# Band attention and a GELU layer on one core: seven-product second layer for two more chunks, f16 scores for three units, 64-row products that subtract the maxima

## The chip, the cores and the metric

The kernel runs on one core of one Trainium2 chip. The metric is the device time of one execution in microseconds (us). A profile gives the span from the first to the last instruction.

## The reference

Attention over 4 batches, 8 heads, 768 positions and 64 dimensions, in which a query sees the keys within 15 positions of its own and one summary key for each block of 32 (the block's maximum, with the mean of the block's values). The output is fed to a two-layer network.

```python
k_sum = k.reshape(B, H, nb, block, D).max(axis=3)
v_sum = v.reshape(B, H, nb, block, D).mean(axis=3)
scores_all = np.concatenate([scores_l_m, scores_s], axis=-1)
scores_all = scores_all - np.max(scores_all, axis=-1, keepdims=True)
a = np.exp(scores_all)
a = a / (np.sum(a, axis=-1, keepdims=True) + 1e-09)
x = np.ascontiguousarray(attn_out.transpose(0, 2, 1, 3)).reshape(B * S, H * D)
h = x @ w_in                                   # 3072 x 512 by 512 x 2048
g = 0.5 * h * (1.0 + erf(h * inv_sqrt2))
return (g @ w_out).astype(np.float32)          # 3072 x 2048 by 2048 x 512
```

## The kernel before

The 3072 tokens are 12 chunks of 256. A chunk's attention is done in two units (24 in all) of 4 heads by 256 queries. An operand that must be exact to more than f16 is split into a high and a low f16 part, and a product is then three f16 products (high by high, high by low, low by high). ScalarE makes the high parts (`*_hi`), VectorE the low parts (`*_lo`), as a subtraction.

Attention of unit u: `scores` (or `f_scores`, with f32 operands; units 0 to 5) multiplies keys and queries, `evac` or `add_mask` brings the scores to SBUF, `maximum` finds the maximum over the 128 partitions on GpSimd, and the maximum is subtracted. That is `shift` (L789) on VectorE, or, for units 0 to 3, `m_shift` (L733) on TensorE: products that add minus the maximum to the scores still lying in PSUM. `exponent` or `m_exponent`, `sums` (denominators), `values`, and the `norm_*` steps follow, and `x_hi`, `x_lo` split the result, the input of the network. For `scores` the keys are split by `s_k_hi` and `k_lo` (L723), the queries by `s_q_hi` and `q_lo` (L728), and the block maxima by `prep_k_end` (L523) and `k_sums`; for `f_scores` ScalarE copies the keys into one f32 tile (`k_pack`).

First layer: chunks 0 to 3 with `phase1` (L908; 24 products of 256 columns a step), and chunks 4 to 11 in pairs (batch "b" = 2 to 5 is chunks 2b and 2b+1) by `sp` (L962), Strassen's seven products instead of eight. Second layer: `phase2` (L1023; 12 products of 512 columns for a quarter of the 2048 rows and 128 tokens). For b = 5 alone (chunks 10 and 11) the second layer is done in seven products too: `so` (L1169), whose left operands are sums of the GELU outputs (`h_sum`, `h_hi`, `h_lo`) and whose right operands are sums of parts of `w_out` (`t_sum`, `t_hi`, `t_lo`).

The weights arrive as raw 64-bit numbers. VectorE turns each of 8 pieces of `w_in` and 8 of `w_out` into f32 in three steps (`wi_bits`, `wo_bits`: L386, L391, L395), and then makes the low part: `wi_lo` (L424), `wo_lo` (L484). `phase1` of column block i needs `wi_lo i`; `phase2` of quarter q needs `wo_lo 2q` and `wo_lo 2q+1`, and the chunk's `g_lo`.

The order of the work on every engine and of the DMAs (all on SP's queue) is a list written out in the source, `ORDER`; each name is a method and its arguments, and each engine executes its own instructions in that order. Steps `fill` are products of ones whose result nobody reads: 14 of three products each, and 16 more products at the start. Tiles of a tag rotate through a number of buffers that the pool hands out in turn.

Of the kernel before, what the change touches and what calls it, by code (L numbers as in the profile page):

```python
# [82 lines left out]
0, wi_bits 2 0, evac 2, load_ind, wi_bits 2 1, fetch_vt 0, sum_vt 0, norm_cross 0, norm_rec 0, maximum 2, fetch_vt 1,
norm_spread 0, m_shift 1, m_exponent 1, fetch_vt 2, load_v 0, sum_vt 1, sum_vt 2, wi_bits 2 2, wi_hi 2, wi_lo 4,
k_pack 3, m_shift 2, fill 12, fetch_w_in 3 3, wi_lo 5, wi_lo 2, wi_bits 3 0, load_v 1, mean_vt, wi_bits 3 1, f_sums 1,
s_load_vs 0, f_values 0, norm_mult 0, m_exponent 2, f_mask 3, load_q 3, f_scores 3, s_load_vs 1, norm_take 1, wi_bits
3 2, x_hi 0, x_lo 0, norm_cross 1, norm_rec 1, f_values 1, fill 13, evac 3, f_sums 2, norm_spread 1, norm_mult 1,
norm_take 2, fetch_w_in 1 1, wi_hi 3, x_hi 1, x_lo 1, fetch_w_out 1 5, norm_cross 2, wi_bits 1 0, norm_rec 2, phase1 0
4, wo_bits 1 0, wi_bits 1 1, load_q 6, maximum 3, m_shift 3, s_q_hi 6, wo_bits 1 1, wi_bits 1 2, phase1 0 2, fetch_k 2
1, prep_k 2 1, load_v 2, m_exponent 3, load_vs 2, wi_hi 1, fetch_w_in 7 3, norm_spread 2, q_lo 6, phase1 0 5, f_values  # L90
2, load_v 3, gelu 0 5, g_hi 0 5, wi_lo 1, load_vs 3, fetch_k 1 3, f_mask 4, wo_bits 1 2, gelu 0 2, load_k 4, g_hi 0 2,
norm_mult 2, k_pack 4, f_sums 3, gelu 0 4, norm_take 3, load_q 4, norm_cross 3, prep_k 1 3, wi_bits 7 0, phase1 0 1,
f_values 3, wi_lo 3, wi_bits 7 1, load_v 4, wo_hi 1, fetch_k 1 2, f_scores 4, x_hi 2, fetch_k 1 1, evac 4, norm_rec 3,
norm_spread 3, g_hi 0 4, prep_k 1 2, gelu 0 1, phase1 0 0, x_lo 2, norm_mult 3, x_hi 3, fetch_w_in 6 2, prep_k 1 1,
f_mask 5, load_vs 4, x_lo 3, g_lo 0 4, g_lo 0 5, fetch_w_out 0 4, fetch_w_out 3 5, wi_bits 6 0, phase1 0 3, maximum 4,
shift 4, wo_lo 1, load_k 5, wi_bits 6 1, g_hi 0 1, g_lo 0 1, gelu 0 0, g_hi 0 0, g_lo 0 0, phase1 1 4, fetch_v 1 2,
load_q 5, gelu 0 3, fetch_k 1 0, phase1 1 5, exponent 4, g_hi 0 3, wi_bits 7 2, f_values 4, gelu 1 5, wo_bits 0 0,
wi_bits 6 2, f_sums 4, g_hi 1 5, g_lo 1 5, wi_hi 7, k_pack 5, wo_bits 0 1, norm_take 4, wi_lo 7, phase1 1 1, load_v 5,
gelu 1 1, g_hi 1 1, g_lo 1 1, wi_hi 6, phase1 1 0, wi_lo 6, prep_v 1 2, load_vs 5, gelu 1 4, f_scores 5, phase1 1 7,
norm_cross 4, gelu 1 0, g_hi 1 0, evac 5, g_hi 1 4, g_lo 0 3, load_k 6, s_k_hi 6, norm_rec 4, wo_bits 0 2, maximum 5,  # L100
norm_spread 4, prep_k 1 0, g_lo 1 0, load_v 6, wo_bits 3 0, fetch_w_out 2 4, phase1 1 6, wo_hi 0, wo_bits 3 1, phase1
1 3, gelu 1 7, phase1 0 7, wo_lo 0, phase2 0 0, shift 5, gelu 1 3, g_hi 1 3, wo_bits 3 2, fetch_w_out 5 5, g_lo 1 3,
norm_mult 4, wo_bits 2 0, exponent 5, f_sums 5, prep_k_end 1 0, f_values 5, gelu 1 6, wo_bits 2 1, load_q 7, norm_take
5, wo_bits 2 2, k_lo 6, g_hi 1 7, g_lo 1 7, wo_hi 3, k_sums 1 0, wo_bits 5 0, wo_lo 3, phase1 0 6, g_lo 0 2, gelu 0 6,
g_hi 0 6, wo_bits 5 1, wo_hi 2, wo_lo 2, fetch_w_out 4 4, f_mask 6, wo_bits 4 0, wo_bits 4 1, norm_cross 5, norm_rec
5, phase1 1 2, gelu 0 7, wo_bits 4 2, wo_hi 4, wo_bits 5 2, wo_hi 5, prep_k_end 1 1, wo_lo 4, wo_lo 5, g_lo 1 4,
scores 6, fetch_v 1 0, phase2 0 1, phase2 0 3, norm_spread 5, load_k 7, s_k_hi 7, phase2 0 2, fetch_v 1 1, phase2 0 5,
g_hi 0 7, fetch_w_out 6 4, x_hi 4, fetch_w_out 7 5, x_lo 4, norm_mult 5, s_q_hi 7, prep_v 1 1, evac 6, maximum 6,
phase2 0 4, load_mask, x_hi 5, x_lo 5, load_v 7, f_mask 7, q_lo 7, gelu 1 2, k_sums 1 1, shift 6, exponent 6, phase1 2
3, g_lo 0 6, wo_bits 6 0, phase1 2 1, load_q 9, k_lo 7, gelu 2 3, wo_bits 7 0, wo_bits 6 1, scores 7, g_hi 1 2, g_lo 1  # L110
2, wo_bits 6 2, wo_bits 7 1, gelu 2 1, s_q_hi 9, wo_hi 6, g_lo 0 7, wo_lo 6, phase1 2 0, load_k 9, wo_bits 7 2, q_lo
9, phase1 2 4, s_k_hi 9, k_lo 9, fetch_v 1 3, gelu 2 0, g_hi 2 0, s_p_hi 6, wo_hi 7, wo_lo 7, phase1 2 6, load_q 11,
load_k 8, phase2 0 6, fetch_k 2 2, prep_v 1 0, g_hi 1 6, g_lo 2 0, s_q_hi 11, prep_v 1 3, q_lo 11, p_lo 6, phase2 0 7,
store 0 0, phase2 1 0, fetch_v 2 1, load_vs 6, load_q 8, evac 7, maximum 7, load_vs 7, s_k_hi 8, gelu 2 6, put 0 0,
g_lo 1 6, prep_v 2 1, sums 6, k_lo 8, fetch_k 2 0, gelu 2 4, g_hi 2 4, v_hi 6, scores 9, norm_take 6, phase2 1 2,
phase2 1 4, prep_k 2 2, shift 7, v_hi 7, v_lo 6, values 6, store 0 1, fetch_k 2 3, g_lo 2 4, g_hi 2 1, prep_k 2 0,
phase1 2 5, s_q_hi 8, q_lo 8, add_mask 9, v_lo 7, scores 8, exponent 7, s_p_hi 7, norm_cross 6, phase2 1 6, p_lo 7,
load_v 8, prep_k 2 3, put 0 1, g_hi 2 6, load_k 11, s_k_hi 11, add_mask 8, load_vs 8, v_hi 8, k_lo 11, norm_rec 6,
norm_spread 6, sums 7, norm_mult 6, x_hi 6, norm_take 7, v_lo 8, phase1 2 2, maximum 9, shift 9, load_q 10, maximum 8,
shift 8, store 1 0, prep_k_end 2 1, values 7, norm_cross 7, norm_rec 7, scores 11, exponent 8, x_lo 6, exponent 9,  # L120
s_q_hi 10, phase2 1 1, load_v 9, norm_spread 7, load_vs 9, gelu 2 5, load_k 10, load_v 11, phase2 1 3, g_lo 2 1,
add_mask 11, load_vs 11, norm_mult 7, g_hi 2 5, g_lo 2 6, s_p_hi 8, p_lo 8, g_hi 2 3, g_lo 2 3, x_hi 7, phase1 2 7,
s_k_hi 10, phase2 1 5, x_lo 7, v_hi 9, maximum 11, phase1 3 0, v_lo 9, gelu 2 7, wt_add 1 0, wt_add 1 1, wt_add 1 2,
wt_hi 1, k_lo 10, sums 8, shift 11, values 8, s_p_hi 9, q_lo 10, norm_take 8, norm_cross 8, load_v 10, gelu 3 0, g_hi
3 0, wt_lo 1, fetch_k 3 1, load_q 12, load_vs 10, norm_rec 8, phase1 3 4, phase2 1 7, wt_add 5 0, p_lo 9, phase1 3 1,
norm_spread 8, norm_mult 8, put 1 0, g_lo 3 0, gelu 2 2, exponent 11, scores 10, wt_add 5 1, fetch_k 3 2, g_hi 2 2,
g_lo 2 2, prep_k 3 1, x_hi 8, store 1 1, wt_add 5 2, g_hi 2 7, g_lo 2 7, gelu 3 4, prep_k 3 2, values 9, wt_hi 5, sums
# [1216 lines left out]
```

## Time and profile before

| | |
|---|---|
| time, median of 3 runs | 576.7 us (575.52 to 577.2) |
| profiled execution, span | 574.3 us; its time is not recorded apart from its span |
| TensorE (PE) busy | 569.0 us, 99% of the span, 5826 products |
| VectorE (DVE) busy | 458.4 us, 80% |
| ScalarE (ACT) busy | 379.8 us, 66% |
| GpSimd (POOL) busy | 88.7 us, 15% |
| granted TensorE clock | 0.999 in the mean |

A product's listed duration is longer than the distance to the next one's start, as products are pipelined: busy times of single products must not be added, the distances of their starts may be. For VectorE the same holds to a smaller degree. The chain of waits is followed back from the last instruction, and names at every moment the work on which the end hung.

### The profile page before, as it was taken

The numbers are of one execution on the slowest core, as the hardware profiler recorded it, in microseconds if no ns is written. First come the engines' busy times: TensorE is split into PE (matmuls) and PEld (weight loads), VectorE is DVE, ScalarE is ACT, GpSimd is POOL, SyncE is SP. The second block draws the span as 40 slices with busy tenths as digits, with TensorE's granted clock in tenths as the row PEclk, the third lists the DMA queues.
The fourth block names the chain that finished last, engine by engine and source line by source line (L and its number), as shares of the span: only waits on it lengthen the run. The fifth ranks groups of instructions, "written<-read, shape, count | busy, mean of one in ns | idle before, by whom it ended". The sixth has DMA issues, their size and how long they took to land.

```text
span 574.3 us, 13533 instructions
## 1 busy us (share of the span) xinstructions
PE 569.0 (99%) x5826; PEld 389.8 (68%) x5826; DVE 458.4 (80%) x617; ACT 379.8 (66%) x642; POOL 88.7 (15%) x42
## 2 busy tenths in 40 slices
PE   9999999999999999999999999999999999999997
PEld 4457887485677565777755676665667756667886
DVE  4899999998999798988888677687556675678863
ACT  3486777666679667877987778774677843456431
POOL 2432340202422020203122220130400000000000
PEclk9999999999999999999999999999999999999999
DMA  8967955736433422342332231132020000000002
GB/s 322 395 238 250 342 175 196 274 116 198 159 115 99 141 79 71 115 121 76 103 93 66 72 105 56 60 98 78 23 63 1 21 19 18 1 20 1 2 1 91
DMA packets 28652, 64.27 MB, mean 112 GB/s; under 512 B 2736, under 2 KB 7600, under 8 KB 28592
## 3 DMA queue, kind: packets, MB, share of 16 engines
q1 hardware_dynamic: 28592, 63.41, 33.5%
q8 instruction: 45, 0.74, 0.5%
q14 instruction: 15, 0.12, 0.1%
HBM read 55.34 MB, written 6.29 MB: 107 GB/s over the span
## 4 chain that ended last, share of the span: by engine, by line
PE 95%; DVE 4%; issue 1%; ACT 0%; POOL 0%; DVEq 0%; ACTq 0%; POOLq 0%
PE psy L986 15%; PE pso L1034 12%; PE pso L1035 12%; PE pso L1036 12%; PE psz L986 7%; PE psh L915 4%; PE psh L917 4%; PE psh L916 4%; PE psx L986 4%; PE pso_y L1199 4%; PE psv L838 3%; PE pss L756 3%; PE pss_x L1199 2%; PE pso_fill L337 2%; PE pss L688 1%; PE pso_fill_s L337 1%
## 5 line engine op out<-in xcount | busy, mean ns | idle before, releaser
L785 POOL PARTITION_ALL_REDUCE m<-s x23 | 77.4, 3370 | 303.5 <-DVE s L776 80.9
L1034 PE MATMUL pso<-w_out_h,gg 128*128 128x512 f16 x320 | 121.5, 380 | 0.0
L1035 PE MATMUL pso<-w_out_l,gg 128*128 128x512 f16 x320 | 121.3, 379 | 0.0
L1036 PE MATMUL pso<-w_out_h,gg 128*128 128x512 f16 x320 | 121.3, 379 | 0.0
L986 PEld LDWEIGHTS <-wt 128*128 128x128 f16 x768 | 74.4, 98 | 13.6 <-issue 1.1
L916 PE MATMUL psh<-xos,ww 128*128 128x256 f16 x256 | 69.8, 273 | 0.6 <-DVE xos L895 0.6
L915 PE MATMUL psh<-xos,ww 128*128 128x256 f16 x256 | 69.9, 273 | 0.0
L917 PE MATMUL psh<-xos,ww 128*128 128x256 f16 x256 | 69.8, 273 | 0.0
L986 PE MATMUL psy<-xos,wt 128*128 128x256 f16 x576 | 69.3, 273 | 0.0
L986 PEld LDWEIGHTS <-ww 128*128 128x128 f16 x576 | 55.4, 98 | 11.7 <-issue 0.4
L1036 PEld LDWEIGHTS <-gg 128*128 128x128 f16 x320 | 31.3, 98 | 37.8
L1034 PEld LDWEIGHTS <-gg 128*128 128x128 f16 x320 | 31.3, 98 | 33.2 <-issue 0.8
L1035 PEld LDWEIGHTS <-gg 128*128 128x128 f16 x320 | 31.3, 98 | 31.5
L1018 DVE SCALAR_TENSOR_TENSOR gg<-g,gg 128x512 f16<-128x512 f32 x48 | 34.7, 731 | 11.5 <-ACT gg L1014 11.4
L997 ACT ACTIVATE ww<-psy 128x512 f32<-128x512 f32 x48 | 28.1, 587 | 23.7 <-PE psy L986 23.4
L1041 ACT ACTIVATE ot<-pso 128x512 f32<-128x512 f32 x20 | 11.8, 592 | 29.3 <-PE pso L1036 29.3
L1014 ACT ACTIVATE gg<-g 128x512 f16<-128x512 f32 x48 | 29.4, 625 | 2.7 <-PE pso L1035 2.0
L1004 DVE TENSOR_TENSOR g<-psz,ww 128x512 f32<-128x512 f32 x24 | 16.4, 682 | 18.5 <-PE psz L986 15.8
L1011 ACT ACTIVATE g<-g 128x512 f32<-128x512 f32 x36 | 22.3, 623 | 10.8 <-DVE g L1004 10.7
L915 PEld LDWEIGHTS <-ww 128*128 128x128 f16 x256 | 25.0, 98 | 6.3 <-issue 2.2
L917 PEld LDWEIGHTS <-ww 128*128 128x128 f16 x256 | 25.0, 98 | 3.7 <-issue 0.7
L916 PEld LDWEIGHTS <-ww 128*128 128x128 f16 x256 | 25.0, 98 | 3.4
(152 smaller groups left out, 1189.5 us busy)
## 6 DMA issues: line engine op xcount, KB each, us to landing
v<-in_vw_dram SPq DMA_DIRECT2D x24, 512.0 KB
k<-in_kd_dram SPq DMA_DIRECT2D x20, 320.0 KB
...
```

Source lines behind the costliest of these rows:

```text
L785: nc.gpsimd.partition_all_reduce(out_ap=self.m32, in_ap=self.s32, channels=P, reduce_op=bass_isa.ReduceOp.max)
L915: nc.tensor.matmul(ph[:, e, :], wh, xh, start=(k == 0), stop=False)
L916: nc.tensor.matmul(ph[:, e, :], wh, xl, start=False, stop=False)
L917: nc.tensor.matmul(ph[:, e, :], wl, xh, start=False, stop=(k == NCC - 1))
L986: nc.tensor.matmul(ps[:, e, :], ws, xx, start=(first and e == 0 and k == 0 and m == 0), stop=(k == 1 and m == 2), skip_group_check=True,)
L997: nc.scalar.activation(snaps[b, q, n], split8(acc[b, q, "y"]), AF.Copy)
L1014: nc.scalar.activation(g_part(o // 2, q, 0, slice(o % 2, 4, 2)), g32t[b, q, o], AF.Copy, scale=SC_G)
L1018: nc.vector.scalar_tensor_tensor(out=g_part(o // 2, q, 1, fs), in0=g32t.pop((b, q, o)), scalar=SC_G, in1=g_part(o // 2, q, 0, fs), op0=ALU ...
L1034: nc.tensor.matmul(p, gh, w_out_h[:, f, :], start=(f == 0), stop=False)
L1035: nc.tensor.matmul(p, gh, w_out_l[:, f, :], start=False, stop=False)
L1036: nc.tensor.matmul(p, gl, w_out_h[:, f, :], start=False, stop=(f == NFC - 1))
L1199: nc.tensor.matmul(ps[:, j, :], g, ww_, start=(first and e == 0 and k == 0), stop=(e == 1 and k == 2), skip_group_check=True,)
```

## The change

The second layer of chunks 8 and 9 (b = 4) is done by `so` as well, so `L2` is now a pair, and the methods take b as an argument. For b = 4 the sums of the GELU outputs lie in free rooms (`s_room`), the row halves of its "y" result in two PSUM tiles, and the sum of `w_out` number 1 is written in place over the part of `w_out` that `so` does not read. Units 3 to 5 use `scores` with f16 parts; units 3 to 5 then use `shift` (before, 4 and 5 did), and `m_shift` stays for units 0 to 2, with 64 rows of minus 1/64 instead of one row of minus 1. Tiles of ten tags take the buffer that a list (`SLOTS`) names. `ORDER` is written anew, with 11 fills instead of 14.

```diff
-L2 = 5
+L2 = (4, 5)
...
+class Slots:
...
+        if bufs > 1 and tag in SLOTS:
+            left = self.left.setdefault(tag, iter(SLOTS[tag].replace("\n", "")))
+            return self.pool.tile(shape, dtype, tag=f"{tag}_{next(left)}", bufs=1, name=name)
...
-            nc.gpsimd.memset(neg_1, -1.0)
+            nc.gpsimd.memset(neg_1, -1.0 / D)
...
-                row, sl = slice(e * D, e * D + 1), slice(e * QCOLS, (e + 1) * QCOLS)
+                rows, sl = slice(e * D, (e + 1) * D), slice(e * QCOLS, (e + 1) * QCOLS)
                 nc.tensor.matmul(
-                    self.halves[e], neg_1[row].broadcast_to([1, P]), self.m32[row, sl],
+                    self.halves[e], neg_1[rows].broadcast_to([D, P]), self.m32[rows, sl],
...
-    def a_part(q, m, z):
+    def s_room(q, m):
...
+    def a_part(b, q, m, z):
...
+        if b == L2[0]:
+            room, i = s_room(q, m), z * 2 * CH
...
     def t_room(q, n, z):
+        if n == 1:
+            return b_part(q, 0, 1, z)
...
-    def so(n, q, j):
+    def so(b, n, q, j):
...
+        key = (b, y, j) if y == "y" else (b, y)
...
+                acc[key] = ps_d.tile([P, CH], F32, tag="psd", name=f"psd_y_{b}") if j else (
+                    ps_o.tile([P, DM], F32, tag="pso", name=f"pso_y_{b}")[:, :CH])
```

Counted over the whole lists, these steps change in number: `phase2` 80 to 64, `so` 56 to 112, `h_hi` and `h_lo` 28 to 56 each, `h_sum` 16 to 32, `sg_hi` and `sg_lo` 48 to 32 each, `o_sum` 4 to 8, `scores` 18 to 21, `f_scores` 6 to 3, `k_lo` and `q_lo` 18 to 21 each, `prep_k_end` 6 to 8, `shift` 20 to 21, `m_shift` 4 to 3, `k_pack` 6 to 3, `fill` 14 to 11. `sp`, `phase1`, `t_sum`, `t_hi`, `t_lo`, `maximum`, `wi_*`, `wo_*` keep theirs.

The list moves nearly every instruction; three places matter here. First, SP's queue at the very start, before:

```order
L510 DMA w_out_l_91<-in_kp_dram 128x2x784
L325 DMA mask16_sb_81<-in_mask16_dram 128x320
L594 DMA q32_0_141<-in_qd_dram 128x512
L371 DMA gg_92<-in_w_in_dram 128x4x512
L510 DMA w_out_l_91<-in_kp_dram 128x2x784
```

and now:

```order
L576 DMA w_out_l_91<-in_kp_dram 128x2x784
L660 DMA q32_0_125<-in_qd_dram 128x512
L391 DMA mask16_sb_81<-in_mask16_dram 128x320
L437 DMA gg_92<-in_w_in_dram 128x4x512
L606 DMA w_out_h_90<-in_vt_dram 128x1024
L394 DMA w_out_l_91<-in_mask_dram 128x272
L576 DMA w_out_l_91<-in_kp_dram 128x2x784
```

The second half of batch 0's keys (the second `in_kp_dram`) has come to stand behind a part of the values (`in_vt_dram`, 512 KB) and the indicator matrix (a part of `in_mask_dram`, 136 KB).

Second, VectorE at the start, where `ks_f` holds the block maxima of the keys and `wt` the first pieces of `w_in`; before:

```order
L519 TENSOR_REDUCE ks_f_84<-w_out_l_91 128x2x24
L386 TENSOR_SCALAR wt_87<-gg_92 128x1024
L391 SCALAR_TENSOR_TENSOR wt_87<-gg_92,wt_87 128x1024
L519 TENSOR_REDUCE ks_f_84<-w_out_l_91 128x2x24
L395 SCALAR_TENSOR_TENSOR wt_87<-gg_92,wt_87 128x1024
L386 TENSOR_SCALAR wt_87<-x32s_88 128x1024
```

and now:

```order
L585 TENSOR_REDUCE ks_f_84<-w_out_l_91 128x2x24
L593 CAST ks16_0_0_128<-ks_f_84 128x48
L594 TENSOR_TENSOR ks16_0_0_128<-ks_f_84,ks16_0_0_128 128x48
L452 TENSOR_SCALAR wt_87<-gg_92 128x1024
L457 SCALAR_TENSOR_TENSOR wt_87<-gg_92,wt_87 128x1024
L585 TENSOR_REDUCE ks_f_84<-w_out_l_91 128x2x24
L790 TENSOR_TENSOR k_all_93<-w_out_l_91,k_all_93 128x10x64
L461 SCALAR_TENSOR_TENSOR wt_87<-gg_92,wt_87 128x1024
L452 TENSOR_SCALAR wt_87<-xos_89 128x1024
```

The splits that f16 scores need (`ks16`, and `k_all` for the low keys of unit 3) stand ahead of or between the steps on the weights.

Third, VectorE up to the low part of the last two pieces of `w_out` (`wst_6` and `wst_7` are their f32 forms); before:

```order
L395 SCALAR_TENSOR_TENSOR wst_6_1399<-xos_89,wst_6_1399 128x1024
L391 SCALAR_TENSOR_TENSOR wst_7_1431<-x32s_88,wst_7_1431 128x1024
L933 SCALAR_TENSOR_TENSOR gg_92<-g32_0_7_1213,gg_92 128x512
L484 SCALAR_TENSOR_TENSOR w_out_l_91<-wst_6_1399,w_out_h_90 128x1024
L395 SCALAR_TENSOR_TENSOR wst_7_1431<-x32s_88,wst_7_1431 128x1024
L730 TENSOR_TENSOR ql_9_1521<-q32_9_1426,qh_9_1488 128x512
L724 TENSOR_TENSOR k_lo1_96<-k32_9_1518,k_hi1_94 128x10x64
L484 SCALAR_TENSOR_TENSOR w_out_l_91<-wst_7_1431,w_out_h_90 128x1024
```

and now:

```order
L457 SCALAR_TENSOR_TENSOR wst_6_1456<-xos_89,wst_6_1456 128x1024
L999 SCALAR_TENSOR_TENSOR gg_92<-g32_2_4_1550,gg_92 128x512
L457 SCALAR_TENSOR_TENSOR wst_7_1519<-x32s_88,wst_7_1519 128x1024
L999 SCALAR_TENSOR_TENSOR gg_92<-g32_1_6_1428,gg_92 128x512
L461 SCALAR_TENSOR_TENSOR wst_6_1456<-xos_89,wst_6_1456 128x1024
L871 TENSOR_TENSOR pl_6_1598<-s32_6_1354,ph_6_1584 128x1024
L634 TENSOR_REDUCE vs_1_1521<-vb_1_1_1589 96x32
L461 SCALAR_TENSOR_TENSOR wst_7_1519<-x32s_88,wst_7_1519 128x1024
L550 SCALAR_TENSOR_TENSOR w_out_l_91<-wst_6_1456,w_out_h_90 128x1024
L550 SCALAR_TENSOR_TENSOR w_out_l_91<-wst_7_1519,w_out_h_90 128x1024
```

The low parts of the two pieces come together at the end, behind low parts of GELU outputs (`g32_2_4`, `g32_1_6`) and of unit 6's weights (`pl_6`), while the splits for unit 9 come after them. The last row shown is the 129th instruction of VectorE before and the 142nd now.

## Rows read from the trace of the kernel before

**Rows 1.** Page: busy time of each engine; shares of the final chain by engine.
```profile
...
PE 569.0 (99%) x5826; PEld 389.8 (68%) x5826; DVE 458.4 (80%) x617; ACT 379.8 (66%) x642; POOL 88.7 (15%) x42
...
PE 95%; DVE 4%; issue 1%; ACT 0%; POOL 0%; DVEq 0%; ACTq 0%; POOLq 0%
```

**Rows 2.** Waits of TensorE: waiter, releaser, total, times, longest.
```profile
...
PE pso_fill_s L337 <- POOL warm L349: 0.9, 1, 0.9
PE psh L916 <- DVE xos L895: 0.6, 1, 0.6
```

**Rows 3.** Windows: busy of PE, PEld, DVE, ACT, POOL, then PEclk, DMA share, GB/s.
```profile
...
42.50:127.30 84.80, 84.63 (x896) 65.68 (x896) 83.01 (x101) 60.37 (x97) 18.73 (x8) 1.00 0.67 226
...
440.00:571.00 131.00, 131.00 (x1080) 95.94 (x1078) 90.82 (x143) 64.92 (x118) 0.00 (x0) 1.00 0.05 17
...
...
10.00:20.00 10.00, 9.55 (x54) 4.31 (x53) 9.90 (x8) 3.96 (x5) 3.22 (x1) 1.00 1.05 390
```

**Rows 4.** Chain of waits in order of time: start, length, work.
```profile
...
0.94 6.56 PE pso_fill_s L337 x16
...
9.24 1.93 PE pss L688 x32
...
26.41 1.88 PE psh_vt L546 x4
...
32.94 1.06 PE pss L736 x4
34.00 0.77 PE pso_fill L337 x3
...
99.75 0.81 PE pss L756 x48
...
555.98 5.24 PE pso_y L1199 x48
```

**Rows 5.** Timeline of TensorE, 88 to 131 us: start, duration, instruction.
```profile
...
100.49 0.39 PE L1034 MATMUL pso<-w_out_h,gg 128*128 128x512 f16 x1
...
113.23 0.38 PE L1036 MATMUL pso<-w_out_h,gg 128*128 128x512 f16 x1
...
127.90 0.38 PE L1034 MATMUL pso<-w_out_h,gg 128*128 128x512 f16 x1
```

**Rows 6.** Timeline of VectorE, first 30 us; in brackets idle before and releaser.
```profile
...
9.09 0.69 DVE L386 TENSOR_SCALAR wt<-gg 128x1024 int32<-128x1024 int32 x1 [2.18 <-DMA gg<-in_w_in_dram]
...
11.07 1.75 DVE L519 TENSOR_REDUCE ks_f<-w_out_l 128x48 f32<-128x1536 f32 x1
...
23.24 0.45 DVE L861 STREAM_TRANSPOSE dent<-psn 128x256 f32<-128x256 f32 x1 [0.61 <-PE psn L710]
...
28.55 0.25 DVE L877 RECIPROCAL rc<-rc 128x16 f32<-128x16 f32 x1 [1.45 <-ACT rc L874]
```

**Rows 7.** Timeline of VectorE, 95 to 127 us.
```profile
...
95.32 0.81 DVE L724 TENSOR_TENSOR k_lo<-k,k_hi 128x640 f16<-128x640 f32 x1
96.05 0.68 DVE L933 SCALAR_TENSOR_TENSOR gg<-g,gg 128x512 f16<-128x512 f32 x1
...
105.52 0.18 DVE L527 CAST ks<-ks 128x48 f16<-128x48 f32 x1
...
105.86 2.35 DVE L484 SCALAR_TENSOR_TENSOR w_out_l<-wst,w_out_h 128x1024 f16<-128x1024 f32 x2
...
113.20 1.22 DVE L790 TENSOR_TENSOR s<-s,m 128x1024 f32<-128x1024 f32 x1
114.34 0.68 DVE L933 SCALAR_TENSOR_TENSOR gg<-g,gg 128x512 f16<-128x512 f32 x1
...
123.81 0.67 DVE L730 TENSOR_TENSOR ql<-q,qh 128x512 f16<-128x512 f32 x1
124.41 0.81 DVE L724 TENSOR_TENSOR k_lo<-k,k_hi 128x640 f16<-128x640 f32 x1
126.04 1.22 DVE L484 SCALAR_TENSOR_TENSOR w_out_l<-wst,w_out_h 128x1024 f16<-128x1024 f32 x1 [0.83 <-ACT w_out_h L481]
```

More of the change, by code (lines that the diff above doesn't have):

```diff
@@ L83 @@
[L83 to L127, printed above, removed]
@@ L218 @@
-2, t_hi 1 3, t_hi 1 1, t_lo 1 1, phase2 9 4, phase2 9 6, put 9 1, t_lo 1 3, t_lo 1 2, t_sum 1 6, t_sum 1 7, h_gelu 1
-2, snap 5 2 1, store 9 0, t_sum 2 3, t_hi 1 4, t_lo 1 4, h_hi 1 22, put 9 0, sp 5 2 6, sp 5 1 3, h_hi 0 3, snap 5 2 2,
-h_lo 0 3, t_sum 2 1, t_sum 2 0, phase2 8 1, t_sum 2 2, h_lo 1 22, t_sum 2 4, h_hi 0 12, t_hi 2 1, h_sum 1 1, h_comb 1
-1, h_hi 0 11, sp 5 2 7, h_lo 0 11, h_gelu 1 1, phase2 8 3, h_lo 0 12, h_hi 1 12, h_sum 0 2, t_hi 2 3, sp 5 3 1, h_hi 0
-2, h_hi 1 11, h_sum 1 3, h_hi 1 3, snap 5 3 1, h_lo 0 1, phase2 8 5, h_lo 1 11, h_sum 1 2, h_lo 1 12, h_hi 1 2, sp 5 2
@@ new lines @@
+xsum 4 2, xs_hi 4 2, xsum 4 4, phase2 6 4, k_lo 23, phase2 6 6, store 6 0, sp 4 0 1, s_gelu 3 3 3, norm_rec 20, xs_lo
+4 2, shift 22, phase2 6 1, sg_hi 3 3 3, load_v 22, load_vs 22, v_hi 22, p_lo 21, norm_spread 20, sp 4 0 2, snap 4 0 1,
+scores 23, exponent 22, norm_mult 20, sums 21, snap 4 1 1, add_mask 23, put 6 0, values 21, maximum 23, sg_lo 3 2 3,
+norm_take 21, h_comb 4 0 0, v_hi 23, sp 4 1 6, phase2 6 3, h_gelu 4 0 0, sp 4 0 6, xs_lo 4 1, phase2 6 5, xs_hi 4 4,
+phase2 6 7, v_lo 23, norm_cross 21, shift 23, norm_rec 21, sg_hi 3 2 2, xs_lo 4 3, sg_hi 3 3 2, snap 4 0 2, sg_lo 3 3
@@ new lines @@
+4 1 0, phase2 7 4, t_hi 0 3, t_lo 0 3, h_gelu 4 0 2, t_sum 0 4, phase2 7 6, t_sum 0 5, sp 4 1 5, t_sum 0 6, t_sum 0 7,
+store 7 0, phase2 7 1, snap 4 1 3, t_hi 0 4, t_hi 0 2, h_comb 4 1 3, t_lo 0 4, t_sum 1 1, h_gelu 4 0 3, sp 4 1 3,
+h_gelu 4 1 0, t_lo 0 2, t_hi 0 1, t_lo 0 1, h_comb 4 1 1, h_hi 4 0 22, h_lo 4 0 22, h_sum 4 0 1, h_hi 4 0 1, sp 4 2 1,
+t_sum 1 0, h_gelu 4 1 1, h_sum 4 0 3, h_hi 4 1 12, sp 4 3 1, sp 4 1 4, t_sum 1 3, t_sum 1 2, t_sum 1 4, t_hi 1 3,
+h_gelu 4 1 2, h_sum 4 0 2, h_lo 4 0 1, phase2 7 3, snap 4 3 1, so 4 2 0 0, phase2 7 5, h_gelu 4 1 3, t_hi 1 1, h_hi 4
@@ new lines @@
+1 11, t_lo 1 3, sp 4 2 2, phase2 7 7, t_sum 1 5, t_sum 1 6, h_hi 4 0 3, h_lo 4 0 3, t_hi 1 2, h_hi 4 1 22, snap 4 2 1,
+t_sum 1 7, h_sum 4 0 4, t_hi 1 4, h_hi 4 0 2, t_lo 1 2, t_lo 1 1, h_lo 4 1 22, t_lo 1 4, sp 4 2 6, h_comb 4 2 0, t_sum
+2 1, put 7 0, t_sum 2 0, h_gelu 4 2 0, t_sum 2 2, h_sum 4 1 1, h_hi 4 2 11, h_hi 4 0 4, snap 4 2 2, h_lo 4 0 4, t_sum
+2 3, h_lo 4 0 2, sp 4 2 5, store 7 1, h_lo 4 2 11, so 4 2 0 1, sp 4 2 7, snap 4 2 3, sp 4 3 6, snap 4 3 2, h_comb 4 2
+3, h_lo 4 1 11, h_lo 4 1 12, sp 4 2 4, sp 4 2 3, put 7 1, h_sum 4 1 3, h_sum 4 1 2, h_hi 4 1 3, h_sum 4 1 4, h_comb 4
@@ new lines @@
+so 5 4 1 1, o_out 5 1, o_put 5 2 1
+'''
+SLOTS = {
+    "f4k": (
+        "0123023232100321213021210320320103210323122021323103132212303012320203012030312101312013032301321023"
+        "103120"
+    ),
+    "g32": (
+        "012300120312130123300120123120321302012312130320210331210231031121300123"
+    ),
+    "ks16": (
+        "01010101"
+    ),
+    "ks32": (
+        "010"
+    ),
+    "psh": (
+        "012012120120120121211212121112010102210212100121210112120200102222021101210020021012"
+    ),
+    "qh": (
+        "01000101001010101000101"
+    ),
+    "ql": (
+        "01000101001010101000101"
+    ),
+    "v32": (
+        "01010110101010110101010101"
+    ),
+    "vh": (
+        "01010101001010001001"
+    ),
+    "vl": (
+        "01010101001010001001"
+    ),
+}
@@ L1199, in so @@
                 nc.tensor.matmul(
-                    ps[:, j, :], g, ww_, start=(first and e == 0 and k == 0), stop=(e == 1 and k == 2),
+                    ps, g, ww_, start=(first and e == 0 and k == 0), stop=(e == 1 and k == 2),
                     skip_group_check=True,
```

405 lines of the change are left out of this document (242 added, 163 removed).

## The prediction

> **What bounds the kernel now.** I read the page first: TensorE is busy 99% of the span, and the chain that ended last lies on it for 95% [rows 1]. The waits of TensorE then show that it is truly fed: 0.9 us at the start and 0.6 us for the first input of the network is all that it waits [rows 2]. So the span is nearly a sum of product distances, and anything taken off TensorE shows, as long as nobody else becomes late. That is asked of the windows: between 42.5 and 127.3 us, where the weights are turned into f16 parts, VectorE is busy 83.0 of 84.8 us; between 440 and 571 it has room, 90.8 of 131 [rows 3]. In the first stretch two engines are full at once. How near they stand is read at the last weights: VectorE makes the low part of the last piece of w_out from 126.04 to 127.26 [rows 7], and the product step that reads it, the third quarter of chunk 0's second layer (`phase2 0 6`), starts at 127.90 [rows 5]. VectorE is ahead by 0.6 us there. That margin decides this case.
>
> **TensorE's sum.** The prices are distances of starts. From 100.49 to 113.23 lie 59 distances of 512-column products: 0.216 us each [rows 5]; 48 products of 256 columns take 5.24 us, 0.109 each [rows 4].
> - Second layer of chunks 8 and 9: 16 steps of `phase2` go, 192 products of 0.216, 41.5 us; 56 steps of `so` come, of 6 products of 0.109, 36.7 us. That is 4.8 us less. Two PSUM tiles for "y" change no count, and the in-place sum of w_out only takes a room.
> - f16 scores of three units: 1.93 us for 32 f32 products against 0.81 for 48 f16 ones [rows 4], 3 x 1.12 = 3.4 us less.
> - Subtraction of unit 3's maximum leaves TensorE: 1.06 us less [rows 4].
> - The same subtraction with 64 rows for units 0 to 2: the columns are the same and the two halves still stand on different rows, so I take no change. The dear bound is the rate of the f32 products on all 128 rows, 1.88 us for four [rows 4]: 0.8 more for each unit, 2.4 in all, and it would fall into a stretch where VectorE sets the pace. Fewer passes than now can't come of more rows, so there is no gain to bound.
> - Three fills: 0.77 each [rows 4], 2.3 less.
>
> Together 11.6 us, a span of 562.7 if nobody waits.
>
> **VectorE up to the last weight.** The f16 scores of units 3 to 5 put on it what f32 scores don't need, all ahead of the last piece of w_out: three low parts of keys of 0.73 us (95.32 to 96.05), three of queries of 0.60 (123.81 to 124.41), two splits of block maxima of 0.34 (105.52 to 105.86), and one subtraction of a maximum of 1.14 (113.20 to 114.34) [rows 7]: 2.2 + 1.8 + 0.7 + 1.1 = 5.8 us. The list also moves two low parts of GELU outputs and unit 6's weights ahead (0.60 + 0.60 + 1.14) and three small splits behind it (0.60 + 0.60 + 0.73), 0.4 more. Nothing leaves VectorE there: what goes with the f32 scores (`k_pack`) was ScalarE's. So 6.2 us are added to an engine that was full.
>
> Its idle time changes too. The second half of the keys was reduced at 11.07, without a wait [rows 6]; its DMA now stands behind 648 KB more, and at the 390 GB/s of that time [rows 3] this is up to 1.7 us of new wait on VectorE. One split (0.3) fits into the 2.18 us in which it waits for the first weights, and the waits of 0.61 and 1.45 [rows 6] and of 0.83 [rows 7] can be filled, as it now has more to do than time: 2.9 at most. I take all of these, 1.7 - 0.3 - 2.9 = -1.5; the ends are -3.2 (the keys land in time) and +1.4 (no wait is filled). The last low part is then ready at 127.3 + 6.2 - 1.5 = 132.0 (130.3 to 134.9), and `phase2 0 6` starts then, 4.1 later than before.
>
> TensorE would like to be there at 127.9 - 6.8 (scores, subtraction, fills) + 2.9 (the list has drawn one more step of chunk 2's first layer, 24 x 0.109, and 0.3 of unit 6's denominators ahead) = 124.0. So it waits 8.0 us in all, in pieces spread over 40 to 130 us: for the split input, for `wi_lo`, `wo_lo` and the keys' low parts. The removed fills hide nothing here: their time becomes waiting. DMAs and GpSimd's 24 maxima keep their number, and GpSimd waits more than it works [rows 1], so I cost their order at nothing; what covers them is the same VectorE lag.
>
> **After the last weight.** What followed took 574.3 - 127.9 = 446.4 us. Of this go 4.8 for the second layer and 2.9 drawn ahead: 438.7. The new second layer adds 12 `h_lo`, 16 `h_sum` and 4 `o_sum` to VectorE, 32 of some 0.60, 19 us, in a stretch with 40 us of room. The tightest piece by the new list: between the product that frees `h_comb 4 3 3` and `so 4 2 3 1` VectorE has 54 instructions, 54 x 0.61 = 32.9 us, and TensorE 16 `sp` and 21 `so`, 16 x 1.31 + 21 x 0.655 = 34.8. It fits with 1.9 us over, though every low part also passes ScalarE first; I put 0.6 us of waits on it (0 to 4.2, below). The end stays as it is: one eviction of 256 columns and its store.
>
> Span: 132.0 + 438.7 + 0.6 = 571.3, 3.0 less than 574.3. The profiled execution's span is 2.4 below the median of the runs, 576.7, which holds what lies around it; the forecast is **573.7 us**.
>
> **The rivals.**
> 1. *VectorE keeps up* (0.22). For it: VectorE's distances in this stretch hold time lost to GpSimd and to waits, and a list with other neighbours may lose less; only few TensorE steps need the last piece. Against: the 6.2 us are instructions, not waits, and 98% busy [rows 3] leaves 1.8. The whole of TensorE's sum comes through: 576.7 - 11.6 + 0.6 = 565.7.
> 2. *VectorE binds a second time at the end* (0.13), slower or no gain. Place: the 35 us above, and the same piece for chunks 10 and 11. If an instruction there costs its whole duration of 0.68 (96.05 [rows 7]) and not its distance, for want of the next being ready, 54 x 0.68 = 36.7 against 34.8, 2 us in each of the two, 4.2 with the ends, on top of the first lag at its late bound (134.9, 2.9 more): 573.7 - 0.6 + 4.2 + 2.9 = 580.2. It decides from the forecast's own lag on: with 1.9 us of such waits (575.0) no gain can be measured, from 5.3 us on (578.4) the kernel is slower.
> 3. *The clock falls in the new waits* (0.05), slower. [...] Waits of 1 to 3 us are new. [...]
>
> **How the numbers follow.** The forecast has 0.60. Within it the bounds of VectorE's idle time give 572.0 to 576.6, and about 0.7 of that lies below 575.0. I call 0.3%, 1.7 us, what a measurement of this kernel can tell from no change. Faster: 0.42 + 0.22 = 0.64; within: 0.17 and a third of rival 2, 0.22; slower: the rest of rival 2, rival 3 and 0.01 of the forecast, 0.14. The range goes from rival 1 with 1.2 us for the error of its sum, 564.5, to the forecast's late bound with 1.4 us more of late waits, 578.0; what is left out is the far part of rivals 2 and 3.
>
> **What would show it.** In the changed profile, waits of TensorE for VectorE that sum to 6 to 10 us between 40 and 133 us, VectorE 98% busy there, the last `wo_lo` ending near 132 and `phase2 0 6` right behind it; from there to the end about 439 us. The 256-column products keep 0.109 and the f16 scores 0.81; 64-row subtractions still take 1.06. If the step starts near 124, rival 1 is right and my VectorE sum wrong; if the last 130 us show waits for `h_lo` or `t_lo` above 2 us, rival 2; a granted clock below 1.00 in the windows of 40 to 130 us, rival 3. The forecast is wrong altogether if the sum of TensorE's products falls by clearly more or less than 11.6 us.

## The result and the profile after

The changed kernel takes 568.54 us in the median of 4 runs (567.24 to 570.79), the kernel before 576.5 us beside it (575.52 to 577.2, 4 runs): a ratio of 0.9868, 95% interval 0.9841 to 0.9895, 8.0 us less. The profiled execution has a span of 565.5 us, 8.8 below that of before; it is the fastest of the four. One execution of a variant below, at a mean granted clock of 0.656, took 816 us and is left out of that variant's times.

The page of the changed kernel: span, busy time of each engine, and shares of the final chain by engine.

```profile
span 565.5 us, 13963 instructions
...
PE 556.4 (98%) x6005; PEld 401.8 (71%) x6005; DVE 473.9 (84%) x660; ACT 386.4 (68%) x667; POOL 94.4 (17%) x42
...
PE 75%; DVE 16%; ACT 5%; issue 2%; POOL 1%; DMA 1%; DVEq 0%; ACTq 0%; POOLq 0%
```

The 179 products more are the counted ones: 144 for the second layer, 48 for the scores, less 4 of the subtraction and 9 of fills. TensorE's share of the chain fell from 95% [rows 1] to 75%, and VectorE has 16% of it. So the end now hangs on VectorE in part. Yet TensorE waits little. Its waits (waiter, releaser, total, times, longest), whole span:

```profile
PE psh L981 <- ACT g L990: 1.4, 3, 0.6
PE pso_fill_s L403 <- POOL warm L415: 0.9, 1, 0.9
PE psz L1052 <- DVE g L1070: 0.7, 1, 0.7
PE psh L982 <- DVE xos L961: 0.7, 2, 0.4
PE pss L802 <- POOL m L851: 0.5, 1, 0.5
```

Many small waits stand where [rows 2] had two. The windows of the two stretches (columns as in [rows 3]):

```profile
42.50:127.30 84.80, 83.36 (x922) 64.74 (x920) 84.46 (x103) 60.83 (x95) 16.61 (x6) 1.00 0.59 202
440.00:563.00 123.00, 122.19 (x1118) 108.99 (x1115) 84.30 (x135) 59.33 (x116) 0.00 (x0) 1.00 0.06 19
```

VectorE is busy 84.46 of 84.8 us ahead of the last weight (83.01 before) and the clock is 1.00 throughout. The last two low parts of `w_out`, in VectorE's timeline, and the start of `phase2 0 6` in TensorE's:

```profile
125.08 2.43 DVE L550 SCALAR_TENSOR_TENSOR w_out_l<-wst,w_out_h 128x1024 f16<-128x1024 f32 x2
```

```profile
126.20 0.38 PE L1100 MATMUL pso<-w_out_h,gg 128*128 128x512 f16 x1
```

VectorE is done at 127.5 us, against 127.26 before [rows 7]: 6.2 us more of instructions cost it 0.2. The step starts 1.7 us earlier than in [rows 5], and 1.3 us before VectorE is done, as its first products need only the first of the two pieces. TensorE does not wait at it. Its last wait ahead of the step is this one, for the low part of a unit's result (`x_lo`, L961):

```profile
110.00 0.27 PE L982 MATMUL psh<-xos,ww 128*128 128x256 f16 x1 [0.30 <-DVE xos L961]
```

From there it works for 16.2 us without a wait, in this trace and in those of eight variants of the changed kernel below (all but the one with `wo_lo` made twice and the one without maxima). The chain followed back goes over to VectorE at 110 us and lies on it for most of the time back to 56 us. So VectorE sets the pace up to 110 us, and the last low parts come just in time.

From the start of the step to the end it takes 565.5 - 126.2 = 439.3 us; before, 446.4.

This last number is a gauge. Seven traces of kernels that share the list behind the step (the changed one and six variants below) give 439.2 to 439.3. So whatever differs between executions of these lists lies ahead of the step, and its start can be had from any execution's span.

### The profile page after: what moved, and what is told of

Read it like the earlier page. It is cut to its first block, busy times and chain, and to the rows that moved or that the text cites. A ratio compares the mean times of both kernels' runs of the same rounds, so it can differ in the third digit from the quotient of the medians.

```text
span 565.5 us, 13963 instructions
## 1 busy us (share of the span) xinstructions
PE 556.4 (98%) x6005; PEld 401.8 (71%) x6005; DVE 473.9 (84%) x660; ACT 386.4 (68%) x667; POOL 94.4 (17%) x42
## 4 chain that ended last, share of the span: by engine, by line
PE 75%; DVE 16%; ACT 5%; issue 2%; POOL 1%; DMA 1%; DVEq 0%; ACTq 0%; POOLq 0%
PE psy L1052 14%; PE pso L1100 8%; PE pso L1101 7%; PE pso L1102 7%; PE psz L1052 7%; PE psd_y L1288 4%; PE pso_y L1288 3%; PE pss_x L1288 3%; PE psx L1052 3%; PE psh L982 2%; PE psh L981 2%; PE psh L983 2%; PE psv L904 2%; PE pss L822 2%; PE psv_z L1288 2%
## 5 line engine op out<-in xcount | busy, mean ns | idle before, releaser
L851 POOL PARTITION_ALL_REDUCE m<-s x23 | 82.6, 3590 | 287.0 <-DVE s L842 128.5
L1100 PE MATMUL pso<-w_out_h,gg 128*128 128x512 f16 x256 | 97.1, 379 | 0.0
L1101 PE MATMUL pso<-w_out_l,gg 128*128 128x512 f16 x256 | 97.0, 379 | 0.0
L1102 PE MATMUL pso<-w_out_h,gg 128*128 128x512 f16 x256 | 97.0, 379 | 0.0
L1102 PEld LDWEIGHTS <-gg 128*128 128x128 f16 x256 | 25.1, 98 | 30.2
L1100 PEld LDWEIGHTS <-gg 128*128 128x128 f16 x256 | 25.0, 98 | 26.1 <-issue 0.2
L1101 PEld LDWEIGHTS <-gg 128*128 128x128 f16 x256 | 25.1, 98 | 25.8
L1288 PEld LDWEIGHTS <-gg 128*128 128x128 f16 x384 | 37.5, 98 | 4.7 <-DVE gg L1180 0.2
L859 ACT ACTIVATE s<-s 128x1024 f32<-128x1024 f32 x21 | 22.2, 1056 | 8.5 <-DVE s L856 8.4
L856 DVE TENSOR_TENSOR s<-s,m 128x1024 f32<-128x1024 f32 x21 | 25.5, 1214 | 0.5 <-POOL m L851 0.5
L999 DVE SCALAR_TENSOR_TENSOR gg<-g,gg 128x512 f16<-128x512 f32 x32 | 25.2, 790 | 0.0
L871 DVE TENSOR_TENSOR pl<-s,ph 128x1024 f16<-128x1024 f32 x18 | 21.8, 1210 | 3.5 <-ACT ph L867 3.5
```

The source lines that it names most:

```text
L851: nc.gpsimd.partition_all_reduce(out_ap=self.m32, in_ap=self.s32, channels=P, reduce_op=bass_isa.ReduceOp.max)
L856: nc.vector.tensor_tensor(out=self.s32, in0=self.s32, in1=self.m32, op=ALU.subtract)
L999: nc.vector.scalar_tensor_tensor(out=g_part(c, i // 2, 1, fs), in0=g32t.pop((c, i)), scalar=SC_G, in1=g_part(c, i // 2, 0, fs), op0=ALU.mu ...
L1100: nc.tensor.matmul(p, gh, w_out_h[:, f, :], start=(f == 0), stop=False)
L1101: nc.tensor.matmul(p, gh, w_out_l[:, f, :], start=False, stop=False)
L1102: nc.tensor.matmul(p, gl, w_out_h[:, f, :], start=False, stop=(f == NFC - 1))
```

## Experiments

Times stand beside the kernel before on the same chip (575.8 to 576.5 in the medians of the four groups of runs).

**VectorE's load doubled in part, in both lists.** The edit, the same in both kernels:

```diff
-            out=wo_part(f, w_out_l), in0=sts.pop(f), ...
+        st = sts.pop(f)
+        for _ in range(2 if f < 6 else 1):
...
+                out=wo_part(f, w_out_l), in0=st, ...
```

In the kernel before:

> The kernel before, with the low part of w_out pieces 0 to 5 made twice: six more VectorE instructions of 1.14 us, 6.8 us, between 67 and 107 us, about what the change adds (6.2). Theory 1 (the prediction's: an added VectorE instruction costs its own duration, and past the margin of 0.6 us and the idle 0.8 us TensorE waits for each of them): the last low part of w_out ends near 133, phase2 0 6 starts there, and the kernel takes 5 to 6 us more, 581.5 to 582.5. Theory 2 (VectorE loses less time elsewhere when its list grows, or TensorE's last step has more room than read): the last low part ends near 129 and the time rises by less than 2 us.

Measured: 582.27 us against 575.81, ratio 1.0102 (1.0076 to 1.0128). `phase2 0 6` starts at 134.87 instead of 127.90, 7.0 us later, and the rest takes 581.3 - 134.87 = 446.4 as before. Theory 1: all of it shows at the step, most of it as waits of TensorE for the earlier low parts.

In the changed kernel:

> The changed kernel with the same six low parts made twice (6.8 us more on VectorE, of these 2.3 behind 92 us). Theory 1 (VectorE sets the pace of the changed kernel up to its last weight, as phase2 0 6 starts at 126.2 with the end of the low part of piece 6): nearly all of it shows, 5.5 to 7 us more, 574 to 575.5. Theory 2 (TensorE reaches that step by its own work and VectorE only keeps up): less than 3 us more, and phase2 0 6 starts before 129.

Measured: 579.45 us, ratio to before 1.0066 (1.0043 to 1.0088), 10.9 us over the changed kernel: more than theory 1. The step starts at 137.06, 10.9 later, and the rest is 439.3. Of the 10.9 us 2.3 lie ahead of the edit: VectorE reaches the first low part of `w_out` at 74.31 us, and at 72.00 in the changed kernel. So 8.6 are left for the edit, still more than its 6.8 us of instructions. Two things stand behind the rest. One is the clock; the window around a wait of this variant (columns as above):

```profile
112.00:116.00 4.00, 2.72 (x6) 0.84 (x6) 3.97 (x3) 2.58 (x4) 3.39 (x1) 0.57 0.00 0
```

TensorE had waited 2.40 us for a low part of `w_out`, and the granted clock of these 4 us is 0.57; the first two products of 512 columns behind the wait start 0.38 us apart (112.47 and 112.85), against 0.216 [rows 5]. The other is that VectorE's steps took longer where GpSimd works, even ahead of 71 us, where nothing is changed. GpSimd's timeline in the changed kernel, and VectorE's beside it:

```profile
35.01 2.06 POOL L691 COPY v<-w_out_h 24x1024 f32<-24x1024 f32 x1 [7.07 <-DMA kp<-in_kp_dram]
37.16 4.11 POOL L851 PARTITION_ALL_REDUCE m<-s  x1
```

```profile
34.96 1.21 DVE L461 SCALAR_TENSOR_TENSOR wt<-gg,wt 128x1024 int32<-128x1024 int32 x1
...
37.00 1.18 DVE L461 SCALAR_TENSOR_TENSOR wt<-gg,wt 128x1024 int32<-128x1024 int32 x1
```

and in the variant, the same instructions:

```profile
34.94 1.10 POOL L693 COPY v<-w_out_h 24x1024 f32<-24x1024 f32 x1 [6.89 <-DMA kp<-in_kp_dram]
37.10 3.22 POOL L853 PARTITION_ALL_REDUCE m<-s  x1 [1.07 <-PE psv L770]
```

```profile
35.06 2.05 DVE L461 SCALAR_TENSOR_TENSOR wt<-gg,wt 128x1024 int32<-128x1024 int32 x1
...
37.95 2.12 DVE L461 SCALAR_TENSOR_TENSOR wt<-gg,wt 128x1024 int32<-128x1024 int32 x1
```

Where VectorE started first (34.96 and 35.01, 37.00 and 37.16), it took its usual time and GpSimd some 0.9 us more; where GpSimd started first (34.94 and 35.06, 37.10 and 37.95), VectorE lost 0.84 and 0.9. In these rows a tenth of a microsecond decides who pays. When VectorE's step began, the copy still had 0.98 us to run (34.94 + 1.10 - 35.06), and VectorE lost 0.84; the maximum still had 2.4 us to run (37.10 + 3.22 - 37.95), and VectorE lost 0.9.

**GpSimd's maxima left out.** Units 0 to 6 get zeros:

```diff
+            if self.u < 7:
+                nc.gpsimd.memset(self.m32, 0.0)
+                return
             nc.gpsimd.partition_all_reduce(
```

> The kernel before, with the maxima of units 0 to 6 left out: GpSimd writes zeros into their tile in place of 3.2 us of work each, so the softmax of these units runs unshifted. Theory 1 (what VectorE's instructions lose against their usual distance ahead of the last weight, about 8.7 us in sum, is lost to GpSimd's operations): of the single losses of 0.7 to 1.7 us those under a maximum go (at 12.7, 24.3, 42.5, 84.6), those under a copy (45.7, 50.3, 76.8) stay; about 3 us are left. Theory 2 (they are lost otherwise, to reads of raw weights that DMAs write or to waits that the trace does not show): the sum stays above 7 us. The time falls by less than 1.5 us in either case, as TensorE is never without work there.

> The changed kernel with the maxima of units 0 to 6 left out in the same way. Theory 1 (GpSimd's operations cost VectorE 4.8 us there, and VectorE sets the pace): VectorE loses about 1.5 us instead of 4.8, the last low part ends 2 to 3 us earlier, near 125, and the time falls by 1.5 to 2.5 us, as the waits of TensorE of about 1.9 us ahead of 126 us go. Theory 2 (TensorE's own work sets the pace): VectorE gets ahead, and the time falls by less than 0.8 us.

Before's variant took 574.71 us in one run, 1.1 less. I sum over VectorE's timeline up to the last low part what an instruction takes over the usual distance of its kind (1.13 for 1024 columns, 0.60 for 512, 0.73 for 640) while GpSimd is at work: 8.7 us before, 3.8 here; counted by distances of starts wherever there is one, 7.8 and 3.4. The four copies still cost 0.83 to 0.85 each; the losses under the maxima of 0.7 to 1.7 us are gone. Theory 1 holds: this time is lost to GpSimd. The changed kernel's variant took 565.39 us in three runs, ratio to before 0.9807 (0.9782 to 0.9832), 3.1 less than the changed kernel: theory 1 in the time, and a little more than its range. No trace of these three runs is there, so it is not shown how much of the 3.1 is VectorE's loss: without the maxima TensorE's waits for them go as well (0.5 us in the changed kernel, up to 2.0 in one piece in some variants).

The same sum in the changed kernel is 5.0 us, 3.7 less than before, with as many maxima and copies (4.5 and 3.3 less by the second count).

**The copies on ScalarE.** `load_vs 2` to `load_vs 5` become `s_load_vs`; in a second variant the copies for units 1 and 2 are moved as well:

```diff
-x_hi 0, load_vs 2, wi_bits 3 0, ... norm_cross 1, s_load_vs 1, x_lo 0, ... s_k_hi 4,
+s_load_vs 1, x_hi 0, wi_bits 3 0, ... norm_cross 1, x_lo 0, ... s_k_hi 4, s_load_vs 2,
```

> The changed kernel with the four copies of value means (units 2 to 5) made by ScalarE in place of GpSimd. Theory 1 (VectorE and GpSimd hold each other up when they meet, now the one, now the other, by about 0.85 us a meeting, and VectorE sets the pace up to its last weight): the four meetings with copies go, VectorE's loss ahead of the last weight falls to under 4 us whatever the execution, ScalarE takes 4 more instructions of about 1.05 us where it has room, and the time falls by 0.5 to 2 us against 568.5. Theory 2 (these losses lie beside TensorE's own work): within 0.5 us of the changed kernel, or slower by up to 1 us for what ScalarE does later.

> The changed kernel with the four copies on ScalarE, and the copy for unit 1 drawn ahead of the high part of unit 0's result, that for unit 2 moved behind the high part of unit 4's keys: in most traces TensorE waited 2.5 to 4.2 us at 36 to 40 us for f_values 1, whose copy stood on ScalarE behind a step that waits for VectorE. Theory 1 (that wait is ScalarE's order): it goes, the clock stays at 1.00 there, phase2 0 6 starts at 125 to 126.2 in every execution, and the time is 566.5 to 567.8 with a spread under 1.5 us. Theory 2 (VectorE's chain to x_lo 1 ends no earlier, so the wait only moves to the first product of phase1 0 0): 568 to 569.

Measured: 568.49 us (568.31 to 569.08), ratio 0.9871 (0.9856 to 0.9885), and 569.11 us (568.65 to 570.82), ratio 0.9889 (0.9872 to 0.9907): neither differs from the median of the changed kernel's four runs. That this change brings nothing isn't shown, however. The variant with 28 low parts made twice (below), which has the changed kernel's list up to `phase2 0 6`, ran beside the first of the two on the same chip; by the gauge its four executions reach the step at 129.3 to 130.9 us, and the four of this one at 127.2 to 128.0. In the trace of the first, VectorE still lost 4.8 us, to the maxima alone, and not under 4: a step now fell behind the start of one and lost 1.69. In the second, TensorE's wait for the copy at 37 us is gone, as expected, but one of 3.49 us ahead of the next unit's `f_values` (`values` with f32 operands) has taken its place, and the first product of `phase1 0 0` came at 43.68 us, against 39.97 in the changed kernel. VectorE's L954, which reads the result of the unit before out of its PSUM tile (`psv`), began at 40.99, behind a step that took 2.00 us while a maximum ran: theory 2, VectorE's chain sets it.

**The fills left out.** The edit makes `fill` do nothing.

> The changed kernel without its 11 fills (33 products of ones, 0.77 us for three, 8.5 us in all). Theory 1 (VectorE sets the pace ahead of the last weight, so TensorE's own time there is free): phase2 0 6 starts within 1 us of 126.2, the time of the fills becomes waiting, the total within 1 us of 568.5. Theory 2 (TensorE sets the pace): 4 to 8 us less. Theory 3 (the clock falls in waits of 1 us and more, as it did with the doubled low parts, where it read 0.59 behind a wait of 2.4 us): granted clock of 0.5 to 0.7 in some windows of 2 us ahead of 45 us, first-layer products at 0.216 instead of 0.109 there, and 1 to 5 us more.

Measured: 570.66 us, ratio 0.9913 (0.9893 to 0.9933), 2.1 us more than the changed kernel's median. Of 8.5 us of TensorE's work nothing came back: theory 1. By the gauge the four executions reach the step at 129.2 to 131.4 us, much like those of the changed kernel's list (126.2 to 130.9, below), so that the variant is slower is not shown. What theory 3 says of the clock does show. Windows of this variant:

```profile
34.00:36.00 2.00, 0.00 (x0) 0.00 (x0) 2.00 (x4) 1.24 (x4) 0.75 (x1) 0.95 1.04 395
36.00:38.00 2.00, 0.38 (x8) 0.39 (x9) 2.00 (x3) 1.93 (x5) 1.31 (x1) 0.50 1.05 397
38.00:40.00 2.00, 2.00 (x38) 1.60 (x36) 1.97 (x4) 1.35 (x2) 0.20 (x1) 0.50 0.85 328
```

TensorE does nothing from 34 to 36 us while VectorE is busy all the time, and behind these 2 us without a product the clock is 0.50.

**The subtraction by one row again.** `neg_1[row].broadcast_to([1, P])` with minus 1.

> The changed kernel with the subtraction of the maximum by one row of minus 1 again instead of 64 rows of minus 1/64 (units 0 to 2). The prediction took no change for it (dear bound 0.8 us a unit): four products at 1.0 to 1.1 us with either, and the time within 0.5 us of 568.5. Rival (64 rows cost up to 2.4 us): the four take 0.3 to 0.8 us less with one row.

Measured: 569.45 us, ratio 0.9895 (0.9858 to 0.9931). The four products, in TensorE's timeline of the changed kernel and of the variant:

```profile
15.82 1.13 PE L802 MATMUL pss<-m,neg 64*128 64x512 f32 x4 [0.49 <-POOL m L851]
```

```profile
15.03 1.13 PE L802 MATMUL pss<-m,neg 1*128 1x512 f32 x4 [0.49 <-POOL m L851]
```

No difference: 64 rows cost nothing. One thing differs beside them: between 18.5 and 21.8 us, behind these products and a wait of 0.49 us, the granted clock was 0.50 in the variant's trace (0.96 in the mean of 0 to 20 us; the three products of a fill took 1.49 us from 20.03), and 1.00 throughout in the changed kernel's (0.83 us for such a fill, from 19.95). Whether the one row has a part in that isn't shown; the kernel before has one-row products too and kept 1.00.

**VectorE's room in the second half.** Low parts of b = 4 are made twice, all 28 or the 7 of quarter 2, or replaced by a copy of the high part:

```diff
+        for _ in range(2 if b == 4 else 1):
...
+        for _ in range(2 if b == 4 and q == 2 else 1):
...
+            nc.vector.tensor_copy(out=a_part(b, q, m, 1), in_=a_part(b, q, m, 0))
```

> The changed kernel with each low part of chunks 8 and 9's GELU outputs made twice: 28 more VectorE instructions of about 0.6 us, 16.8 us, between 390 and 490 us. VectorE's busy time there: 44.2 of 52 us (388 to 440), 38.2 of 40 (440 to 480), 28.6 of 40 (480 to 520). Theory 1 (the prediction's count: 1.9 us over in the tightest piece of 35 us): TensorE waits 3 to 8 us for the low parts, 572 to 577. Theory 2 (VectorE's work there is done well ahead, and its 95% busy share is only work drawn forward): under 1.5 us more. Theory 3 (VectorE is already the bound in 440 to 480): 10 us more and over.

> The changed kernel with only the seven low parts of chunk pair 4's third quarter made twice: 7 more VectorE instructions of 0.6 us, 4.2 us, between 442 and 469 us. In four traces of kernels that share the list behind it, the time from phase2 0 6 to the end is 439.2 to 439.3 us, so a change of 0.2 us can be read there. Theory 1 (the prediction's: 1.9 us over in that piece): 441.5, that is 2.3 more. Theory 2 (VectorE's and TensorE's work are both without room there, as 28 low parts made twice cost 16.3 of 16.8 us): 443 to 443.5. Theory 3 (there is buffer in the finished low parts, and only the large dose ran it dry): under 440.3.

> The changed kernel with chunk pair 4's 28 low parts replaced by f16 copies of the high parts, so that these products get the high part twice: VectorE's instruction of about 0.6 us becomes a shorter one, and 6 to 12 us of its work between 390 and 490 us go. Theory 1 (TensorE sets the pace from phase2 0 6 on, VectorE just keeps up): 439.3 becomes 438.5 to 439.3. Theory 2 (VectorE sets the pace in 440 to 480 and TensorE's busy share of 99% hides small waits): 437 or less.

Measured, from the start of `phase2 0 6` to the end, against 439.3: with 28 twice 586.5 - 130.9 = 455.6, 16.3 more for 16.8 us of instructions, a little of it the clock's (0.96 in the mean of 440 to 480 us; behind a wait of TensorE of 2.39 us, 12 products of 256 columns take 2.40 us from 470.55, 0.20 each against 0.109) (588.06 us, ratio 1.0204, 1.0186 to 1.0221); with 7 twice 573.5 - 130.2 = 443.3, 4.0 more for 4.2 (574.97 us, ratio 0.9978, 0.9963 to 0.9993); with copies 569.0 - 130.0 = 439.0, 0.3 less (570.08 us, ratio 0.9899, 0.9878 to 0.9920). Windows 440 to 480 us of the changed kernel, and of the variant with copies:

```profile
440.00:480.00 40.00, 39.67 (x365) 35.40 (x363) 38.21 (x63) 25.99 (x50) 0.00 (x0) 1.00 0.02 8
```

```profile
440.00:480.00 40.00, 39.94 (x358) 34.80 (x356) 31.38 (x62) 25.49 (x48) 0.00 (x0) 1.00 0.02 8
```

VectorE freed of 7 us in this window gains TensorE only its last 0.3; VectorE loaded with 4 us costs 4. Both are full there and neither waits much. That is theory 3 for the 28, theory 2 for the 7, and theory 1 for the copies.

**One fetch moved.** On SP's queue:

```diff
-evac 1, load_q 2, fill 8, fetch_w_in 5 5,
+evac 1, fetch_w_in 5 5, load_q 2, fill 8,
```

> The changed kernel with one name moved: the fetch of w_in's sixth piece ahead of the load of unit 2's queries on SP's queue, where that load waits for its buffer (issued at 11.4 us in the profile of the changed kernel, the fetch at 11.8). In that profile VectorE waited 0.35 us for this piece, at 21.0 us, and its second step on it, at 23.6, stood ahead of GpSimd's maximum at 24.5 and lost nothing; in eight other traces with the same list the piece came at 21.9 to 22.4, and in seven of these the step stood behind the maximum's start and lost 1.69 us. Theory 1 (the landing of this piece decides who waits for whom, and with it most of the changed kernel's spread of 567.2 to 570.8): VectorE starts on it ahead of 21 us in the profile, the second step loses under 0.5 us, and the median is 566.5 to 568 with a spread under 2 us. Theory 2 (other meetings make up for it, or the queries of unit 2, which then land some 2.6 us later, near 21 us, hold up f_scores 2): 568 to 570 with a spread as before.

(The text counts seven of eight; the traces show six of eight.) Measured: 568.96 us (567.71 to 570.39), ratio 0.9874 (0.9854 to 0.9894): theory 2. VectorE did start on the piece at 20.36, and the step that had lost 1.69 lost nothing; but the first step on it then met another maximum and lost 1.34, three meetings between 35 and 44 us went against VectorE for 2.6 more, and TensorE waited 0.8 us for the queries of unit 2. No variant's median is clearly below that of the changed kernel's four runs, save that of the one that leaves the maxima out.

## Why the prediction was right, and where it was wrong

The direction was right, and the time lies in the range; the middle, 573.7 us, is 5.2 too high. A part of that is luck: four runs are few for this kernel. Three variants (28 and 7 low parts twice, and the copies of high parts) have the changed kernel's own list up to `phase2 0 6`; with the changed kernel that makes 22 executions. Their spans less the rest of their own trace put the step at 126.2 to 130.9 us, in the median at 129.7; the four timed ones of the changed kernel give 126.2, 126.4, 128.5 and 129.6. With 129.7 the kernel would take 129.7 + 439.3 + 1.8 = 570.8 us, 2.9 below the forecast. (The 1.8 is what lies around the span in every run, 1.7 to 1.9; the prediction had 2.4 for it.) I can't say how far the chips differ in this, as the runs were on several.

- **TensorE's sum** held in the main. Product counts are as counted, and the subtraction kept its 1.0 to 1.1 us. TensorE's busy time fell by 12.6 us, where the sum gave 11.6. What follows the last weight takes 439.3 us, just the 438.7 and 0.6 of the forecast, but that it agrees to 0.1 is luck: TensorE waits 2.2 us there and not 0.6, and the distances of its products fell by 9.0 us and not by 7.7.
- **The step that failed** is VectorE's time to the last low part and what hangs on it: "The last low part is then ready at 127.3 + 6.2 - 1.5 = 132.0 (130.3 to 134.9), and `phase2 0 6` starts then". In the profile it was ready at 127.5, and the step started at 126.2. The added instructions are there (VectorE's trace has 131 up to that point before, not 129, and 142 now: 6.2 us by the same prices) and the idle time fell by 1.3 (from 11.4 to 10.1 us) as the 1.5 said. What I had left standing is the time that VectorE loses: 6.2 - 1.3 - 0.2 = 4.7 us of it must have gone, and 3.7 are found under GpSimd's operations; the last 1.0 is not traced. I had priced this loss as a property of the stretch; it is decided anew at each meeting, and in the profile the draw was good. The last low parts in the three variants that share the list up to there:

```profile
129.78 2.42 DVE L550 SCALAR_TENSOR_TENSOR w_out_l<-wst,w_out_h 128x1024 f16<-128x1024 f32 x2
129.12 2.43 DVE L550 SCALAR_TENSOR_TENSOR w_out_l<-wst,w_out_h 128x1024 f16<-128x1024 f32 x2
128.86 2.44 DVE L550 SCALAR_TENSOR_TENSOR w_out_l<-wst,w_out_h 128x1024 f16<-128x1024 f32 x2
```

  They are ready at 132.2, 131.5 and 131.3 us, where the forecast put them, and VectorE loses 7.8 to 7.9 us to GpSimd in them by the second count, as much as before. So VectorE's sum fits these three and not the profile. What fails in all four is that the step starts then: TensorE starts it 1.3 us before, without a wait, as its first products need only the first of the two pieces. The prediction left that out.
- **The forecast's mechanism** held: an added microsecond on VectorE costs one (7.0 for 6.8 in the old list), and TensorE waits for it in pieces, ahead of 110 us. TensorE came to the step 126.2 - 124.0 = 2.2 us behind its own sum in the profile instead of 8.0, and 4.4 to 6.9 behind it in most of the other executions.
- **Rival 1** (VectorE keeps up, 565.7) is near where the best executions go (567.24). Its argument, that a list with other neighbours may lose less to GpSimd, names what the profile shows.
- **Rival 2** did not come, but its place is at its limit. "It fits with 1.9 us over" is wrong: 4.2 us more cost 4.0, so less than 0.3 was over.
- **Rival 3** did not show in the profile, where the longest wait of TensorE is 0.9 us and the clock 1.00. By its own sign, a granted clock below 1.00, it is there in most other executions, in a small size. Of the 18 executions with the list of the change (without the four of the variant with 28 low parts twice, where the clock fell again later), three have a mean clock of 1.0, and these reach the step at 126.2 to 126.4; the other 15 have 0.997, and in the traces of the variants with 7 low parts twice and with copies the fall is at 42.8 and 38.2 us. The kernel before stayed at 0.999 and above. How much of the later step is the clock's and how much the waits' is not separated. That it makes the kernel slower than before, with the chance of 0.05, was the author's estimate; no run shows it. The executions of the changed kernel (567.24 to 570.79 us) all lie below those of the kernel before (575.52 to 577.2), and the traces show the lower clock for a few microseconds at a time: from 43.90 to 46.01 us in the variant with 7 low parts twice, products of 256 columns stand 0.21 us apart instead of 0.109. In the variant with 7 low parts twice, ahead of any edit (waits of TensorE between 20 and 127 us, and a window):

```profile
PE psv L768 <- ACT v L684: 2.3, 1, 2.3
PE psv L768 <- POOL m L851: 2.0, 1, 2.0
```

```profile
42.00:46.00 4.00, 3.68 (x42) 2.98 (x43) 3.89 (x6) 3.78 (x9) 1.67 (x1) 0.59 0.98 373
```

- **Fills**: "The removed fills hide nothing here: their time becomes waiting" is borne out by the 11 that are left: without them, too, nothing came back, and the clock was at 0.50 for a while.
